# One list-scheduled table for all operations, 64-row projection tiles, Q maxima by a transposing VectorE maximum, and turns by DMA

## The chip, the cores and the metric

The kernel runs on one core of one Trainium2 chip. A core has a matrix engine (TensorE, PE in the profile, with its weight loads shown apart as PEld), a vector engine (VectorE, DVE), a scalar engine (ScalarE, ACT), a general engine (GpSimd, POOL) and a queue engine (SyncE, SP). Each runs its own instructions in order and waits for the others through semaphores. SP and POOL also issue the DMA transfers here; POOL's can change the type on the way, and are used for loads that turn float32 into bf16. Matmul results go to PSUM, eight banks of 128 partitions by 512 float32; everything else lives in SBUF.

The metric is device time in microseconds (us), the median of the runs. Three runs of the kernel before gave 429.13, 429.68 and 428.81.

## The reference

```python
def _attn_ref(q, k, v, w_phi):            # q, k, v: (8 batches, 8 heads, 576 rows, 64)
    def phi(x):                            # w_phi: (64, 128)
        proj = np.einsum('bhsd,df->bhsf', x, w_phi)
        proj = proj - np.max(np.abs(proj), axis=-1, keepdims=True)
        return np.concatenate([np.exp(proj), np.exp(-proj)], axis=-1)
    q_p, k_p = (phi(q), phi(k))
    kv = np.einsum('bhsf,bhsd->bhfd', k_p, v)
    z = np.sum(k_p, axis=2)
    num = np.einsum('bhsf,bhfd->bhsd', q_p, kv)
    den = np.einsum('bhsf,bhf->bhs', q_p, z)[..., None] + 1e-06
    return num / den

def _moe_ref(x, w_gate, w_val, w_out):     # x: (4608, 512), widths 1536
    gate = np.maximum(x @ w_gate, 0.0)
    val = x @ w_val
    return gate * val @ w_out
```

The attention's output, heads side by side, is the input x of the second part (called FFN below). All arrays are float32 in DRAM; the kernel multiplies in bf16.

## The kernel before, in words

**Tiles.** Of the 576 rows of a head, 512 form four chunks of 128 (row p*4+c is partition p of chunk c). The last 64 rows of two neighbouring batches are stacked into one "mixed" tile of 128 partitions. So there are 8 batches of 4 chunks and 4 mixed tiles, 36 x tiles of 128 rows in all, which the FFN takes in 9 groups of 512 rows: one for each batch, and a ninth, `xT_mix`, of the mixed rows.

**Keys.** `k_item` handles one pair of heads. Four 128x128 blocks of k (two chunks of 64 columns side by side) are transposed on PE against `ident` (line 131) and copied out of PSUM by DVE (135). `project_rows` (142) multiplies each transposed block by the 128x256 matrix `w2`, which holds w_phi twice on its diagonal, so that one matmul of 256 columns projects two chunks; half of the products are with zeros. DVE takes the largest absolute value of each row (147, one instruction for 512 columns), ACT makes exp(+proj) and exp(-proj) (177, 512 columns each) and exp of the maxima (184). The maximum isn't subtracted; it scales v instead (`scale_v`, 159 and 165, on POOL). `k_kv` (218) sums k_p^T times [v, 1] over the four chunks and the mixed tile: 20 matmuls of 65 columns for each pair of heads. The mixed tile's foreign half is cut off by `half` (194).

**Queries.** `q_item_chunks` handles two chunks of all heads, `q_item_mixed` a mixed tile. The transposed q (131) is projected twice: by rows through `project_rows`, for nothing but the maxima (142, 147), and by columns in `q_cols` (241), 512 columns to a matmul, for the values that ACT exponentiates into `qp` (247). `q_num` (263) multiplies these by kv in three groups of 3, 3 and 2 heads, 65 columns to a matmul; t = second half times exp(2 max) (279 on DVE, 275 on ACT for two chunks of batch 0), u = first half + t (287), a reciprocal (290), and POOL's product `xu` (292). `q_finish` transposes `xu` on PE (299) and DVE copies it to `xT` (305).

**FFN.** `ffn_slices` yields, for each of 12 blocks of 128 hidden columns, a "val" and a "gate" step of four 512-column matmuls each (320), then 12 "out" steps of four (342). ACT copies val out (329), DVE makes relu(gate) times val (331), ACT copies the output (352) and SP stores it (355; 359 for the mixed group). Group 0 does its first six blocks in halves of 256 columns. One such step of four 512-column matmuls is called a quad below.

**Order.** Every function is entered in a list with a tick, by hand-written formulas, and the list is sorted; an engine does its instructions in that order. Attention of a batch runs about one batch ahead of the FFN, so the last two groups (batch 7 and the mixed one) run with no attention beside them. PSUM is split: five banks for attention (`pa`), three for the FFN (`pf`). POOL issues the loads of k, q and the weights, SP those of v from batch 2 on, and the stores.

```python
        for i in range(2):
            nc.tensor.matmul(
                pp[:, 2 * F * i : 2 * F * (i + 1)],
                lhsT=T2[:, i, :],
                rhs=w2.rearrange("p a f -> p (a f)"),
            )
```

Of the kernel before, what the change touches and what calls it, by code (L numbers as in the profile page):

```python
# [8 lines left out]
FP32 = mybir.dt.float32  # L9
# [3 lines left out]
AX = mybir.AxisListType  # L13


@with_exitstack
def kernel(
# [11 lines left out]

    nc = tc.nc
    B, H, S, D = q.shape
    F = w_phi.shape[1]
    NTOK, DM = out.shape  # L40
    DFF = moe_w_gate.shape[1]
    P = 128
    C = 4
    SF = C * P
    SM = S - SF
    NU = H // 2
    NFC = DFF // P
    NDC = DM // P
    E = D + 1

    ctx.enter_context(nc.allow_low_precision("bf16 matmuls"))
    ctx.enter_context(nc.allow_non_contiguous_dma("strided loads"))

    singles = ctx.enter_context(tc.tile_pool(name="singles", bufs=1))
    sb_in = ctx.enter_context(tc.tile_pool(name="sb_in", bufs=1))
    sb_mix = ctx.enter_context(tc.tile_pool(name="sb_mix", bufs=1))
    sb_T = ctx.enter_context(tc.tile_pool(name="sb_T", bufs=3))
    sb_f = ctx.enter_context(tc.tile_pool(name="sb_f", bufs=3))
    sb_k = ctx.enter_context(tc.tile_pool(name="sb_k", bufs=5))
    sb_kv = ctx.enter_context(tc.tile_pool(name="sb_kv", bufs=14))  # L60
    sb_s = ctx.enter_context(tc.tile_pool(name="sb_s", bufs=6))
    sb_x = ctx.enter_context(tc.tile_pool(name="sb_x", bufs=2))
    sb_h = ctx.enter_context(tc.tile_pool(name="sb_h", bufs=2))
    sb_g = ctx.enter_context(tc.tile_pool(name="sb_g", bufs=4))
    ps_a = ctx.enter_context(tc.tile_pool(name="ps_a", bufs=5, space=bass.MemoryType.PSUM))
    ps_f = ctx.enter_context(tc.tile_pool(name="ps_f", bufs=3, space=bass.MemoryType.PSUM))

    ctx.enter_context(tc.manual_schedule())

    def psum_a(dtype=FP32):  # L70
        n = 512 if dtype == FP32 else 1024
        return ps_a.tile([P, n], dtype, name="pa", tag="pa")

    def psum_f():
        return ps_f.tile([P, 512], FP32, name="pf", tag="pf")

    def load_kqv(b, name, src, eng, dtype, heads):

        t = inputs.get((name, b))
        if t is None:
            t = inputs[name, b] = sb_in.tile([P, H, C, D], dtype, name=f"{name}{b % 2}")
        eng.dma_start(
            out=t[:, heads],
            in_=src[b, heads, 0:SF, :].rearrange("h (p c) d -> p h c d", c=C),
        )

    def load_mixed(i, name, src, eng, dtype):
        t = inputs[name, i] = sb_mix.tile([P, H, D], dtype, name=name)  # L90
        for bb in range(2):
            eng.dma_start(
                out=t[SM * bb : SM * (bb + 1)],
                in_=src[2 * i + bb, :, SF:S, :].rearrange("h p d -> p h d"),
            )

    def load_k(b, lo=0, hi=H):
        load_kqv(b, "kn", k, nc.gpsimd, BF16, slice(lo, hi))

    def load_q(b, lo=0, hi=H):  # L100
        load_kqv(b, "qn", q, nc.gpsimd, BF16, slice(lo, hi))

    def load_v(b, lo=0, hi=H, eng=nc.sync):
        load_kqv(b, "vn", v, eng, FP32, slice(lo, hi))

    inputs = {}
    wg_sb = singles.tile([P, NDC, DFF], BF16)
    wv_sb = singles.tile([P, NDC, DFF], BF16)
    wo_sb = singles.tile([P, NFC, DM], BF16)
    xT_mix = singles.tile([P, NDC, SF], BF16)  # L110
    NS = 3
    SPLIT = NFC // 2

    def load_val_gate(t, w, i):
        n = DFF // NS
        nc.gpsimd.dma_start(
            out=t[:, :, n * i : n * (i + 1)],
            in_=w.rearrange("(c p) n -> p c n", p=P)[:, :, n * i : n * (i + 1)],
        )

    def load_out():
        nc.gpsimd.dma_start(out=wo_sb, in_=moe_w_out.rearrange("(c p) n -> p c n", p=P))

    def transposed(blocks):

        n = len(blocks)
        pt = psum_a(BF16)
        for i, blk in enumerate(blocks):  # L130
            nc.tensor.matmul(  # L131
                pt[:, P * i : P * i + P], lhsT=blk, rhs=ident, is_transpose=True
            )
        t = sb_T.tile([P, n, P], BF16, name=f"tT{n}")
        nc.vector.tensor_copy(t.rearrange("p a b -> p (a b)"), pt[:, 0 : n * P])
        return t

    def project_rows(T2, m):

        pp = psum_a()  # L140
        for i in range(2):
            nc.tensor.matmul(  # L142
                pp[:, 2 * F * i : 2 * F * (i + 1)],
                lhsT=T2[:, i, :],
                rhs=w2.rearrange("p a f -> p (a f)"),
            )
        nc.vector.tensor_reduce(  # L147
            m,
            pp.rearrange("p (c f) -> p c f", f=F),
            axis=AX.X,  # L150
            op=ALU.max,
            apply_absolute_value=True,
        )
        return pp

    def scale_v(engs, dst, src, ek):

        for s, eng in enumerate(engs):
            eng.tensor_tensor(
                dst[:, :, s, 0:D],  # L160
                src,
                ek[:, :, s : s + 1].to_broadcast([P, 8, D]),
                op=ALU.mult,
            )
        engs[0].tensor_copy(dst[:, :, :, D], ek)

    def k_start(st, blocks, pool):
        st["T"] = transposed(blocks)
        st["pool"] = pool
        st["kp"] = []  # L170
        st["m"] = sb_s.tile([P, 8], FP32, name="mk")

    def k_rows(st, i):
        pp = project_rows(st["T"][:, 2 * i : 2 * i + 2], st["m"][:, 4 * i : 4 * i + 4])
        kp = st["pool"].tile([P, 2, 4, F], BF16, name=f"kp{i}")
        for s, sign in ((0, 1.0), (1, -1.0)):
            nc.scalar.activation(
                kp[:, s].rearrange("p c f -> p (c f)"), pp, AF.Exp, scale=sign
            )
        st["kp"].append(kp)  # L180
        if i == 1:
            ek = st["ek"] = sb_s.tile([P, 8, 2], FP32, name="ek")
            for s, sign in ((0, -1.0), (1, 1.0)):
                nc.scalar.activation(ek[:, :, s], st["m"], AF.Exp, scale=sign)

    def k_values(st, b, u, engs):
        vs = st["vs"] = sb_k.tile([P, 8, 2, E], BF16, name="vs")
        vn = inputs["vn", b][:, 2 * u : 2 * u + 2].rearrange("p h c d -> p (h c) d")
        scale_v(engs, vs, vn, st["ek"])

    def k_values_mixed(st, i, bb, engs):

        ekm = sb_s.tile([P, 8, 2], FP32, name="ekm")
        nc.vector.tensor_scalar(
            ekm.rearrange("p a b -> p (a b)"),
            st["ek"].rearrange("p a b -> p (a b)"),
            half[:, bb : bb + 1],
            None,
            op0=ALU.mult,
        )  # L200
        vs = st["vs", bb] = sb_mix.tile([P, 8, 2, E], BF16, name=f"vsm{bb}")
        scale_v(engs, vs, inputs["vm", i], ekm)

    def k_kv(st, b, u, copy):
        mixed = km_state[b // 2]
        pk = psum_a()
        kv_ps = pk[:, 0 : 4 * E].rearrange("p (h s e) -> p h s e", h=2, s=2)
        n = 0
        for hh in range(2):
            h = 2 * u + hh  # L210
            for s in range(2):
                for c in range(C + 1):
                    if c < C:
                        lhsT, rhs = st["kp"][hh][:, s, c, :], st["vs"][:, 4 * hh + c, s, :]
                    else:
                        lhsT = mixed["kp"][h // 4][:, s, h % 4, :]
                        rhs = mixed["vs", b % 2][:, h, s, :]
                    nc.tensor.matmul(  # L218
                        kv_ps[:, hh, s, :], lhsT=lhsT, rhs=rhs, start=(n == 0), stop=(n == 19)
                    )  # L220
                    n += 1
        kv = kvs[b, u] = sb_kv.tile([P, 2, 2, E], BF16, name="kv")
        copy(kv.rearrange("p h s e -> p (h s e)"), pk[:, 0 : 4 * E])  # L223

    def q_start(st, blocks):
        st["T"] = transposed(blocks)
        st["m"] = sb_s.tile([P, 2 * len(blocks)], FP32, name=f"mq{len(blocks)}")

    def q_rows(st, i):
        project_rows(st["T"][:, 2 * i : 2 * i + 2], st["m"][:, 4 * i : 4 * i + 4])  # L230
        if 4 * i + 4 == st["m"].shape[1]:
            st["c"] = sb_s.tile(st["m"].shape, FP32, name="cq")
            nc.scalar.activation(st["c"], st["m"], AF.Exp, scale=2.0)
# [374 lines left out]
```

## Time and profile before

| what | value |
|---|---|
| median of three runs | 429.13 us |
| the profiled execution's span, first to last instruction | 426.3 us |
| PE busy (matmuls with their pipeline time) | 398.7 us, 3357 matmuls |
| DVE busy | 284.1 us, 641 instructions |
| ACT busy | 250.9 us, 575 instructions |
| POOL busy | 159.6 us, 204 instructions |
| first matmul; first FFN matmul; end of the last matmul | 4.46; 31.52; 421.73 us |
| granted TensorE clock, mean | 0.998 |

A matmul's recorded time includes its way through the array, so the recorded times of neighbours overlap. What a matmul costs PE in a row of them is read from the starts in the timeline instead. Where a table of the profile says "idle before", it is the time that the engine stood still just ahead of those instructions, and behind the arrow is what ended the wait.

### The profile page before, as it was taken

The numbers are of one execution on the slowest core, as the hardware profiler recorded it, in microseconds if no ns is written. First come the engines' busy times: TensorE is split into PE (matmuls) and PEld (weight loads), VectorE is DVE, ScalarE is ACT, GpSimd is POOL, SyncE is SP. The second block draws the span as 40 slices with busy tenths as digits, with TensorE's granted clock in tenths as the row PEclk, the third lists the DMA queues.
The fourth block names the chain that finished last, engine by engine and source line by source line (L and its number), as shares of the span: only waits on it lengthen the run. The fifth ranks groups of instructions, "written<-read, shape, count | busy, mean of one in ns | idle before, by whom it ended". The sixth has DMA issues, their size and how long they took to land.

```text
span 426.3 us, 8695 instructions
## 1 busy us (share of the span) xinstructions
PE 398.7 (94%) x3357; PEld 232.9 (55%) x3416; DVE 284.1 (67%) x641; ACT 250.9 (59%) x575; POOL 159.6 (37%) x204
## 2 busy tenths in 40 slices
PE   3777899989999999999999999999999999999995
PEld 1556665645556556555566556555565554444442
DVE  4888569867687679866876699676856795330420
ACT  3984776566667755687567665766667552322321
POOL 8953861176217501574155211870362021000000
PEclk9999999999999999999999999999999999999999
DMA  8997795245413750167015901374020002002004
GB/s 157 199 265 164 108 181 61 75 122 59 56 51 98 128 61 2 61 156 94 2 59 160 116 3 52 71 139 51 26 76 2 1 14 86 2 0 100 0 2 98
DMA packets 45337, 33.66 MB, mean 79 GB/s; under 512 B 12848, under 2 KB 40112, under 8 KB 45296
## 3 DMA queue, kind: packets, MB, share of 16 engines
q0 software_dynamic: 30480, 16.52, 28.1%
q1 hardware_dynamic: 14816, 16.58, 12.4%
q8 instruction: 27, 0.44, 0.4%
q14 instruction: 14, 0.11, 0.1%
HBM read 37.81 MB, written 9.44 MB: 111 GB/s over the span
## 4 chain that ended last, share of the span: by engine, by line
PE 78%; DVE 10%; ACT 4%; POOL 2%; issue 2%; DMA 2%; POOLq 0%; DVEq 0%; ACTq 0%
PE pf L320 40%; PE pf L342 17%; PE pa L142 6%; PE pa L218 5%; PE pa L263 4%; PE pa L241 3%; PE pa L131 3%; DVE u L287 2%; DVE mk L147 2%; DMA qn_117<-in_q_dram 2%; DVE t L279 2%; PE pa L299 1%; POOL xu L292 1%; ACT qp L247 1%; ACT t L275 1%
## 5 line engine op out<-in xcount | busy, mean ns | idle before, releaser
L320 PE MATMUL pf<-xT,wv_sb 128*128 128x512 bf16 (+1 forms) x386 | 96.9, 366 | 3.8 <-DVE xT L305 2.6
L320 PE MATMUL pf<-xT,wg_sb 128*128 128x512 bf16 (+1 forms) x394 | 97.7, 366 | 2.0 <-ACT val_sb L329 1.4
L292 POOL TENSOR_TENSOR xu<-u,r 128x512 bf16<-128x512 f32 x36 | 37.5, 1042 | 164.1 <-DVE r L290 128.9
L329 ACT CAST val_sb<-pf 128x512 bf16<-128x512 f32 (+1 forms) x114 | 65.3, 573 | 52.7 <-PE pf L320 52.3
L247 ACT ACTIVATE qp<-pa 128x512 bf16<-128x512 f32 x128 | 69.5, 604 | 11.9 <-PE pa L241 11.9
L320 PEld LDWEIGHTS <-wg_sb 128*128 128x128 bf16 x456 | 44.4, 98 | 41.6 <-issue 2.1
L320 PEld LDWEIGHTS <-wv_sb 128*128 128x128 bf16 x456 | 43.3, 98 | 36.5 <-issue 3.9
L147 DVE TENSOR_REDUCE mk<-pa 128x4 f32<-128x512 f32 x72 | 48.4, 682 | 11.3 <-PE pa L142 11.1
L263 PEld LDWEIGHTS <-qp 128*128 128x128 bf16 x640 | 33.9, 98 | 21.5 <-issue 0.9
L287 DVE TENSOR_TENSOR u<-pa,t 128x195 f32<-128x195 f32 (+3 forms) x120 | 40.5, 338 | 6.8 <-ACT t L275 0.5
L279 DVE TENSOR_TENSOR t<-pa,cq 128x195 f32<-128x195 f32 (+3 forms) x114 | 37.6, 330 | 4.6 <-PE pa L263 3.8
L352 ACT COPY out_sb<-pf 128x512 f32<-128x512 f32 x36 | 21.3, 592 | 32.4 <-PE pf L342 29.5
L263 PE MATMUL pa<-kv,qp 128*128 128x65 bf16 x640 | 37.9, 193 | 0.9 <-DVE u L287 0.5
L331 DVE SCALAR_TENSOR_TENSOR h_6277<-pf,val_sb 128x512 bf16<-128x512 f32 x12 | 8.3, 692 | 22.8 <-PE pf L320 22.8
L331 DVE SCALAR_TENSOR_TENSOR h_6056<-pf,val_sb 128x512 bf16<-128x512 f32 x12 | 8.3, 692 | 14.5 <-PE pf L320 14.5
L299 PEld LDWEIGHTS <-xu 128*128 128x128 bf16 x144 | 10.7, 98 | 11.7 <-POOL xu L292 3.8
L223 ACT CAST kv<-pa 128x260 bf16<-128x260 f32 x28 | 10.7, 380 | 10.0 <-PE pa L218 9.9
L299 PE MATMUL pa<-ident,xu 128*128 128x128 bf16 x144 | 14.0, 219 | 2.1 <-POOL xu L292 1.6
L331 DVE SCALAR_TENSOR_TENSOR h_566<-pf,val_sb 128x256 bf16<-128x256 f32 (+1 forms) x18 | 9.1, 506 | 8.8 <-ACT val_sb L329 4.1
L331 DVE SCALAR_TENSOR_TENSOR h_1578<-pf,val_sb 128x512 bf16<-128x512 f32 x12 | 8.3, 691 | 9.6 <-ACT val_sb L329 5.7
L305 DVE COPY xT<-pa 128x512 bf16<-128x512 bf16 x32 | 13.3, 417 | 1.9 <-PE pa L299 1.7
L331 DVE SCALAR_TENSOR_TENSOR h_3132<-pf,val_sb 128x512 bf16<-128x512 f32 x12 | 8.2, 686 | 7.3 <-PE pf L320 3.8
(580 smaller groups left out, 776.1 us busy)
## 6 DMA issues: line engine op xcount, KB each, us to landing
out_dram<-out_sb SPq DMA_DIRECT2D x32, 256.0 KB, 2.3
wv_sb<-in_moe_w_val_dram POOLq DMA_DIRECT2D x3, 512.0 KB, 8.2
wg_sb<-in_moe_w_gate_dram POOLq DMA_DIRECT2D x3, 512.0 KB, 9.7
wo_sb<-in_moe_w_out_dram POOLq DMA_DIRECT2D x1, 1536.0 KB, 13.3
vn_1018<-in_v_dram SPq DMA_DIRECT2D x1, 1024.0 KB, 8.9
vn_335<-in_v_dram POOLq DMA_DIRECT2D x1, 1024.0 KB, 13.5
vn_1793<-in_v_dram SPq DMA_DIRECT2D x1, 1024.0 KB, 7.1
vn_2508<-in_v_dram SPq DMA_DIRECT2D x1, 1024.0 KB, 7.2
```

What stands on the lines that cost most here:

```text
L142: nc.tensor.matmul(pp[:, 2 * F * i : 2 * F * (i + 1)], lhsT=T2[:, i, :], rhs=w2.rearrange("p a f -> p (a f)"),)
L147: nc.vector.tensor_reduce(m, pp.rearrange("p (c f) -> p c f", f=F), axis=AX.X, op=ALU.max, apply_absolute_value=True,)
L247: nc.scalar.activation(x["qp"][:, s, slot].rearrange("p a b -> p (a b)"), pf, AF.Exp, scale=sign)
L263: nc.tensor.matmul(pn[:, E * (2 * i + s) : E * (2 * i + s + 1)], lhsT=x["qp"][:, s, slot, blk, :], rhs=kvs[b, h // 2][:, h % 2, s, :],)
L279: nc.vector.tensor_tensor(t, ab[:, :, 1], st["c"][rows, col(lo) : col(lo + n - 1) + 1 : col(1) - col(0)][:, :, None].to_broadcast([np_, n, ...
L287: nc.vector.tensor_tensor(x["u"][rows, lo : lo + n], ab[:, :, 0], t, op=ALU.add)
L292: nc.gpsimd.tensor_tensor(x["xu"], x["u"][:, :, 0:D], r.to_broadcast([P, 8, D]), op=ALU.mult)
L299: nc.tensor.matmul(pt[:, P * i : P * i + P], lhsT=x["xu"][:, 2 * i : 2 * i + 2].rearrange("p a d -> p (a d)"), rhs=ident, is_transpose=True,)
L320: nc.tensor.matmul(ps, lhsT=w[:, dc, P * fi : P * fi + P], rhs=xT[:, dc, lo:hi], start=(dc == 0), stop=(dc == NDC - 1),)
L329: nc.scalar.copy(st["val"], ps)
L331: nc.vector.scalar_tensor_tensor(st["h2"][:, fi, lo:hi], ps, 0.0, st["val"], op0=ALU.max, op1=ALU.mult)
L342: nc.tensor.matmul(st["po"], lhsT=st["h2"][:, fi, P * t : P * t + P], rhs=wo_sb[:, fi, :], start=(fi == 0), stop=(fi == NFC - 1),)
```

## The change

The schedule by ticks is gone. A class `Plan` lists all 1774 operations with a number each; a table `ORDER` gives the order in which they are emitted, and `BANKS` the PSUM bank of each. PSUM is no longer split: four tiles of two neighbouring banks each, given out bank by bank or as a pair. What is computed is the same. The parts:

- **Projections in 64-row tiles.** `wd` holds w_phi once in partitions 0 to 63 and once more in 64 to 127. A projection multiplies only the 64 partitions of one chunk, so the two chunks of a block become two matmuls on separate halves of the rows of the array, which write to the two banks of a pair. They are emitted in turns (first half, second half). For k these are 8 matmuls of 128 columns for each of 36 items, in place of 4 of 256. For q they are 2 of 512 columns for each of 32 visits, in place of 4 of 512 for two visits' worth; batch 0 keeps the full-height `w2` (8 matmuls of 512). Two k items, two q visits, or one of each are done in one go: there are 37 such goes (`tile_visit`).
- **Wider evacuation.** Exponentials and maxima now read both banks of a pair in one instruction: 144 exponentials of 1024 columns (before: 288 of 512) and 36 k maxima of 1024 (before: 72 of 512).
- **Q maxima.** The projection of q by rows (144 matmuls of 256 columns, 72 maxima of 512) is gone. In its place DVE takes the column projection itself: 36 `tensor_reduce` instructions over 1024 columns with `apply_transpose`, which turn each 32x32 square and reduce over 32 features. Behind it a float32 transpose of 128x128 on PE (`CT`, 22), a small DVE maximum over the four parts (`CM`), a DVE transpose (`CX`), and ACT's exp (`CE`).
- **Turns by DMA.** From batch 2 on, k and q of a batch (512 KB of bf16 each) are transposed by one SP DMA each, SBUF to SBUF (12), and so are the x tiles of batches 2 to 7 and three mixed ones (27 of 128 KB). PE keeps 112 bf16 transposes, and batch 0's k comes in as float32 and is transposed as such (20 with the mixed tile). In the table 13 to 21 FFN quads lie between a k turn and its first use, 20 to 34 for q, and 5 to 10 between the last x turn of a batch and the first FFN matmul that reads it.
- **The start.** Batch 0's k and v come on SP's queue as float32, in six pieces, with the mixed k and v among them; POOL's loads wait until the third k piece has landed. Batch 0's q comes in two halves. Group 0 of the FFN works on single chunks of 128 and on 256 columns.
- **Smaller things.** `scale_v` does both signs in one instruction; the mixed tile's v is scaled into rows that were zeroed once, so `half` and line 194 go. The t of line 275 moves from ACT to DVE (`NUM_T`), batch 0's `xu` to DVE. `osb` has 2 buffers (before: 3), xT 3 (2). A v load on SP is let go by a one-element POOL memset into its buffer (`go`).
- **Order.** FFN group b and the attention of batch b+1 are interleaved; behind the last attention matmul the table has the last 11 out quads of group 6, then all of group 7 and of the mixed group.

```diff
+TURNED = (0, 1)
...
+FIRST_SP = (
+    ("kf", 0), ("phi",), ("kf", 1), ("kf", 2), ("kf", 3), ("vf", 0), ("kmf", 0), ("vf", 1), ("vm", 0),
+)
+FIRST_POOL = (
+    ("qn", 0, 0), ("wv", 0), ("wg", 0), ("qn", 0, 1), ("wv", 1), ("wg", 1), ("kn", 1), ("wv", 2), ("wg", 2),
+    ("vn", 1), ("q", 1), ("wo", 0), ("wo", 1), ("wo", 2), ("qm", 0),
+)
+GATE = 2
...
+X_BY_DMA = [(b, c) for b in range(2, B) for c in range(C)] + [("m", i) for i in range(1, B // 2)]
...
+def FFN_PARTS(g, fi):
+    if g == 0:
+        return ((0, 1), (1, 2), (2, 4)) if fi < 6 else ((0, 2), (2, 4))
+    return ((0, 4),)
...
+    def turn(self, tag, src, b):
+        t = self.take(tag, (tag, b), [P, 2 * H, P], BF16)
+        self.nc.sync.dma_start_transpose(out=t, in_=self.has[src, b].rearrange("p h c d -> p (h c d)"))
...
+    def k_rows(self, key):
...
+        w = self.pair((key, "p"))
...
+        for i in range(4):
+            for par in range(2):
+                rows = slice(D * par, D * (par + 1))
+                lo = 512 * par + F * i
+                self.nc.tensor.matmul(w[:, lo : lo + F], lhsT=T[rows, i, :], rhs=self.wd[rows, :])
...
+    def q_cols(self, key, v):
...
+        for par in range(2):
+            rows = slice(D * par, D * (par + 1))
...
+            self.nc.tensor.matmul(
+                w[:, 512 * par : 512 * par + 512].rearrange("p (a b) -> p a b", b=P),
+                lhsT=self.wd[rows, :],
+                rhs=rhs,
+            )
...
+        self.nc.vector.tensor_reduce(
+            dst, src, axis=AX.X, op=ALU.max, apply_absolute_value=True, apply_transpose=True
+        )
...
+    def c_turn(self, key):
+        self.nc.tensor.matmul(
+            self.bank((key, "pc"))[:, 0:P], lhsT=self.has[key, "R"], rhs=self.ident_f, is_transpose=True
+        )
...
+    def c_max(self, key):
+        M = self.take("M", (key, "M"), [P, 32], FP32)
+        self.nc.vector.tensor_reduce(
+            M, self.bank((key, "pc"))[:, 0:P].rearrange("p (f t) -> p t f", f=4), axis=AX.X, op=ALU.max
+        )
...
+    def c_back(self, key):
+        MT = self.take("MT", (key, "MT"), [P, 32], FP32)
+        self.nc.vector.transpose(MT, self.has[key, "M"])
...
+    def x_by_dma(self, xk):
+        self.nc.sync.dma_start_transpose(
+            out=self.x_place(xk), in_=self.has[xk, "xu"].rearrange("p h d -> p (h d)")
+        )
...
+    ops = Plan().ops
+    banks = iter(BANKS)
+    for i in ORDER.split():
+        o = ops[int(i)]
+        for _, key in o.psum:
+            emit.bank_of[key] = int(next(banks))
+        getattr(emit, o.call[0])(*o.call[1:])
```

## The prediction

> **What bounds the kernel.** First the engines' busy time and the chain of work that ended last:
>
> ```profile
> PE 398.7 (94%) x3357; PEld 232.9 (55%) x3416; DVE 284.1 (67%) x641; ACT 250.9 (59%) x575; POOL 159.6 (37%) x204
> ...
> PE 78%; DVE 10%; ACT 4%; POOL 2%; issue 2%; DMA 2%; POOLq 0%; DVEq 0%; ACTq 0%
> ```
>
> PE is busy nearly always and carries the chain. Then the stretches before the first FFN matmul, up to 60 us, up to the end of attention, and the rest (length, then busy time by engine):
>
> ```profile
> 0.00:31.50 31.50, 18.48 (x198) 12.66 (x201) 21.58 (x49) 22.70 (x63) 24.40 (x37) 1.00 1.13 204
> 31.50:60.00 28.50, 24.26 (x282) 18.71 (x284) 19.96 (x48) 19.29 (x53) 19.54 (x26) 1.00 0.89 152
> 60.00:355.00 295.00, 289.52 (x2575) 171.44 (x2623) 224.07 (x516) 189.03 (x428) 114.60 (x142) 1.00 0.35 68
> 355.00:427.00 72.00, 66.41 (x306) 30.05 (x310) 18.53 (x30) 19.92 (x34) 1.04 (x1) 0.98 0.14 41
> ```
>
> Between 60 and 355 us PE is idle 5.5 us of 295, so there a matmul less is its time less; DVE has 76%. In the first 31.5 us PE waits for loads and short chains. Now the price of each matmul, from the timeline of PE (start, length, line): starts, not lengths, count.
>
> ```profile
> 136.88 0.29 PE L218 MATMUL pa<-vs,kp_2254 128*128 128x65 bf16 x4
> ...
> 137.48 0.38 PE L142 MATMUL pa<-w_119,tT_2359 128*128 128x256 bf16 x2
> 137.70 1.03 PE L320 MATMUL pf<-xT,wv_sb 128*128 128x512 bf16 x4
> 138.57 0.38 PE L142 MATMUL pa<-w_119,tT_2359 128*128 128x256 bf16 x2
> ...
> 139.65 0.61 PE L131 MATMUL pa<-ident,qn_1874 128*128 128x128 bf16 x8
> 140.10 0.81 PE L320 MATMUL pf<-xT,wv_sb 128*128 128x512 bf16 x3
> ```
>
> Twenty 65-column matmuls of kv took 0.60 us (0.030 each; those of `q_num`, six in 0.19, 0.032), two of 256 columns 0.22 (0.109), four of 512 0.864 (0.216, mean of such rows), eight transposes 0.45 (0.056). PE's demand before: FFN 1296 x 0.216 = 279.9; transposes 432 x 0.056 = 24.2; row projections 288 x 0.109 = 31.4; column projections 72 x 0.216 = 15.6; kv 640 x 0.030 = 19.2; num 640 x 0.032 = 20.5. Sum 390.8. The span of 426.3 has 35.5 more: by 31.5 us some 11.4 of work are done (36 transposes, 36 row and 7 column projections, 80 kv, 32 num, 8 x transposes), so 20.1 are lost at the start; 4.6 pass after the last matmul; 10.8 lie between.
>
> **PE's new demand.** Row projections of q (144 x 0.109) vanish. FFN, kv and num stay: 319.6. Bf16 transposes: 112 x 0.056 = 6.3. The 42 float32 ones aren't in the trace: below, 0.056 as for bf16 of the same shape; above, 0.216, the longest row; I take twice 0.056, being nearest to the same shape with twice the bytes: 4.7 (2.4 to 9.1). Projections in half-height tiles aren't there either: if the halves run side by side, k costs 36 x 4 x 0.056 = 8.1 and q 32 x 0.216 = 6.9; if one after the other, 16.1 and 13.8. I take side by side, since they use different rows and different banks. Batch 0's 8 full ones: 1.7. Sum 347.3, so 43.5 less than before (bounds 345 to 367).
>
> A second price is the change of tiling, 37 goes, in and out: 74 times. Below: nothing. Above: the array runs empty, 379 ns (a 512-column matmul alone) less 216 (in a row) = 163 ns, 12.1 us. I take half, 6.0, having no row nearer to either end. The Trainium skill speaks against this change here: "TensorEngine Tiling (Array Packing)", Key Properties, says that changing the tiling mode drains the engine. No run here shows it; by that rule the forecast would be 6 us later, without it 6 earlier.
>
> **DVE and ACT.** The groups by shape:
>
> ```profile
> L147 DVE TENSOR_REDUCE mk<-pa 128x4 f32<-128x512 f32 x72 | 48.4, 682 | 11.3 <-PE pa L142 11.1
> L247 ACT ACTIVATE qp<-pa 128x512 bf16<-128x512 f32 x128 | 69.5, 604 | 11.9 <-PE pa L241 11.9
> L287 DVE TENSOR_TENSOR u<-pa,t 128x195 f32<-128x195 f32 x64 | 23.0, 361 | 4.6 <-ACT t L275 0.5
> L331 DVE SCALAR_TENSOR_TENSOR h_566<-pf,val_sb 128x256 bf16<-128x256 f32 x12 | 5.0, 419 | 5.6 <-ACT val_sb L329 4.1 <-PE pa L299 0.8 <-PE pa L142 0.7
> L331 DVE SCALAR_TENSOR_TENSOR h_3878<-pf,val_sb 128x512 bf16<-128x512 f32 x12 | 8.2, 685 | 6.5 <-PE pf L320 4.3 <-ACT val_sb L329 1.6 <-PE pa L131 0.6
> ```
>
> DVE takes 266 ns for 256 more columns, 1.04 ns each, so a maximum of 1024 costs 682 + 512 x 1.04 = 1214 ns, against two of 682. The turning one isn't in the trace: below, 1214; above, twice that, if each square is passed twice. I take 1214, the row of the same operation on the same operand. DVE after: maxima 72 x 1.214 = 87.4; gates 96 x 0.685 + 18 x 0.419 + 12 x 0.29 (by the slope) = 76.8; t and u 80 x 0.713 + 40 x 0.575 = 80.0; copies of transposed blocks 28 x 0.417 + 4 x 0.69 = 14.4; reciprocals 7.3; `CM` and `CX` 22 x 0.5 (estimate: 128 and 32 columns on the same slope) = 11; kv copies, batch 0's xu and v 8.5. Sum 285: unchanged, since what the copies save goes into t, xu and the small steps. ACT: an exponential of 512 costs 69.5/128 = 543 ns in a row, one of 1024 543 + 512 x 0.773 (594 and 396 ns for vals of 512 and 256) = 939, so 144 x 0.939 = 135 against 288 x 0.543 = 156; about 229 in all. POOL's products are as many elements as before; its loads and the memsets leave it far under half.
>
> These hide under PE, but less well. After attention come 83 quads, 71.7 us of PE alone. In the 313 us ahead of them (the forecast's) DVE has 285 less 24 x 0.685 = 269, 86% against 76%.
>
> **The DMA turns** of k, q and x aren't in the trace. Rows of like size:
>
> ```profile
> vn_1793<-in_v_dram SPq DMA_DIRECT2D x1, 1024.0 KB, 7.1
> ...
> out_dram<-out_sb SPq DMA_DIRECT2D x8, 128.0 KB, 2.4
> ...
> vm<-in_v_dram SPq DMA_DIRECT2D x6, 128.0 KB, 6.9
> ...
> qn_1099<-in_q_dram POOLq DMA_DIRECT2D x1, 512.0 KB, 10.0
> ```
>
> (KB, then us from issue to landing.) A 512 KB turn: 3.6 (half of 7.1) to 10.0 us, I take 7; 13 quads ahead of the first use are 11.2 us, so nothing waits. A 128 KB x turn: 2.4 to 6.9, against 5 to 10 quads, 4.3 to 8.6 us. At 6.9 groups 2, 3, 6 and 7 start 1.7, 2.6, 0.9 and 1.7 late, 7 us in all; at 2.4 nothing; I take 3.5. On SP's queue a k turn also waits for its load, which is issued 4 to 10 quads (3.5 to 8.6 us) earlier and lands after 6 to 8; behind it stand the q turn and the next x turns and stores, for some 3 us, and an out copy with only two buffers waits for a store. That is hidden while x turns keep their slack; without it the x figures grow by the same 3 us in the groups named.
>
> **The start.** SP brings 2560 KB, at the 204 GB/s of the first window 12.8 us alone; with q's first half and the first weights beside it (another 2560 KB) 25. I take 17 for the last piece, the mixed v. From its product to the first FFN matmul took 9.1 us before (22.4 to 31.5); the new chain has the same steps but the t on ACT, I take 8. First FFN matmul at 25 (21 to 31); PE has done 9.4 by then (20 float32 transposes 2.2, 5 goes 1.1, 16 transposes 0.9, kv 2.4, 6 projections 1.3, num 1.0, the rest 0.5), so 15.6 are lost (11 to 20).
>
> **The sum.** PE 347.3; changes of tiling 6.0; start 15.6; idle between, 10.8 x 86/76 = 12.2 plus 3.5 for late x, 16 (10.8 to 25); after the last matmul 4.6. A span of 389.5. The median before stands 2.8 above the profiled span (429.13 less 426.3), so **392**. All low ends: 345 + 0 + 11 + 10.8 + 4.6 + 2.8 = 374. All high ends, with the halves side by side: 352 + 12 + 20 + 25 + 4.6 + 2.8 = 416.
>
> **Rivals.**
> *Halves one after the other* (PE serialises tiles): + 8.0 + 6.9, 407. For it: nothing in the trace runs two matmuls at once. Against: different rows, different banks.
> *DVE becomes the bound* (the turning maximum takes twice): 36 x 1.214 = 43.7 more, 313 of DVE in attention's 313. DVE stood idle 9.9 us of the first 31.5 and 8.5 up to 60, so that phase takes some 331, and the whole 331 + 71.7 + 4.6 + 2.8 = 410. For it: its chains already ended PE's waits (u, t, mk in the chain). Against: half the price is taken by no other reduce here.
> *The turns bind, slower than before.* SP's turns run one behind the other, three 512 KB for each of batches 2 to 7 (k, q, four x). Attention's phase may last until 429.1 - 2.8 - 4.6 - 71.7 = 350 before the gain is gone; (350 - 60) / 6 = 48 us to a batch, so from 16 us a turn (32 GB/s) the kernel is slower; at 21 us it is 60 + 6 x 63 + 79 = 517. For it: a new kind of transfer, and DMA is busy only in bursts now. Against: the slowest 512 KB row is 10.0. The Trainium skill bears on this: "VectorE: DVE Perf Modes", The three transpose paths, gives 1309 ns for a 128x128 bf16 block by DMA. An estimate by it, 16 blocks in sequence, is 21 us, which would make it slower; no run here shows it, and the sum goes by the rows.
> *The order misses*, engines in order on wrong guesses: idle between doubles to 32, 408.
>
> **How the numbers follow.** Forecast 0.55 (its own range 374 to 402); halves in sequence 0.10; DVE 0.13; order 0.08; turns 0.10 (over 429); a better start and no stalls, under 374, 0.04. The range 374 to 418 leaves out the turns, that last case and a share of DVE's. A difference under 0.2% can't be told from none: faster 0.88, same 0.01, slower 0.11.
>
> **What would show it.** Right: row projections by q gone, starts of paired matmuls a few ns apart, idle PE between 60 us and the end of attention near 4%, DVE near 86% there, first FFN matmul near 25 us, 512 KB turns landing within 10 us. Wrong: PE idle behind DMA turns at each group's first matmul; DVE without gaps; 160 ns holes around each go; a maximum of q over 2 us.

## The result, and the profile after

The changed kernel takes 474.79 us (median; 472.42 to 475.97). The kernel before, run beside it, takes 429.4. The ratio is 1.104, interval 1.0995 to 1.1083: 45 us slower, where 37 faster was forecast.

The profile after: busy time by engine, and the chain of work that ended last.

```profile
PE 388.3 (82%) x3234; PEld 207.3 (44%) x3234; DVE 265.2 (56%) x574; ACT 242.3 (51%) x430; POOL 147.3 (31%) x171
...
PE 41%; DVE 12%; ACT 11%; issue 3%; DVEq 0%; ACTq 0%
```

Every engine has less to do than before (PE 398.7, DVE 284.1, ACT 250.9) and the span is longer: no engine has become the bound. The chain can be followed back only to 154 us here, so its shares add up to 67% of the span; of that part PE has some 60%, DVE 18 and ACT 16 (before: PE 78, DVE 10 and ACT 4 of 98%). The stretches up to 60 us, up to the last attention matmul, and the rest (start and end, length, busy time of PE, PEld, DVE, ACT and POOL, then granted clock, DMA share and GB/s):

```profile
0.00:60.00 60.00, 36.61 (x418) 28.68 (x419) 44.38 (x101) 27.21 (x53) 24.77 (x38) 0.77 0.98 170
60.00:392.00 332.00, 276.69 (x2490) 146.57 (x2488) 202.34 (x442) 193.96 (x342) 120.45 (x131) 1.00 0.51 92
392.00:473.00 81.00, 74.98 (x331) 32.03 (x329) 18.43 (x32) 21.10 (x36) 2.09 (x2) 0.98 0.15 43
```

In the middle stretch, where PE was idle 5.5 us of 295 before, it is now idle 55.3 of 332 (17%; forecast 4%). All other engines have gaps there too: DVE is busy 61% of it, ACT 58%. So no engine is busy throughout, and each waits for others. Which waits? From the list of waits (engine and line <- what ended the wait: us in total, times, longest):

```profile
ACT val L988 <- PE W L976: 77.4, 67, 4.2
...
PEld L976 <- issue: 47.6, 88, 1.8
...
DVE mk L716 <- ACT kp L730: 31.8, 16, 5.0
...
ACT qp L860 <- DVE R L854: 18.9, 16, 5.9
DVE R L854 <- ACT qp L860: 17.3, 17, 3.7
ACT val L988 <- DVE u L932: 13.9, 7, 3.7
ACT kp L730 <- DVE mk L716: 13.4, 12, 1.3
PE W L976 <- DVE h L993: 13.4, 21, 1.1
ACT osb L1015 <- DVE u L932: 11.0, 3, 4.9
```

Two kinds stand out. The maxima (`mk`, `R`) and the exponentials (`kp`, `qp`) wait for each other, in both directions. And ACT's copy `val` of an FFN result, like its copy `osb` of the output, waits for `u`, a DVE sum of the attention. These share no data. One such wait, first on DVE's timeline (start, length), then on ACT's (in brackets the wait ahead of it):

```profile
190.23 0.81 DVE L932 TENSOR_TENSOR u<-W,t 128x195 f32<-128x195 f32 x3
```

```profile
190.96 0.59 ACT L988 CAST val<-W 128x512 bf16<-128x512 f32 x1 [3.65 <-DVE u L932]
```

The copy starts as the third sum ends, having stood 3.65 us. What the two have in common is in the code: `bank()` hands out halves of four two-bank tiles. If dependences between instructions are recorded by PSUM tile, an instruction on one bank waits for earlier ones on its neighbour. The built program has such waits: of the semaphore waits between two of PE, ACT and DVE, 354 are for an instruction that touches only the other bank of the tile and shares no other data (238 of them PE's); in the kernel before, where each buffer is a tile of its own, there are none.

That gives theory 1, false waits between the two banks of a tile. Theory 2: the waits come from the wide readers, which occupy both banks of a pair while exponential, maximum and exponential take turns. Theory 3: the fixed order doesn't fit the durations, whatever the tiles.

### The profile page after: what moved, and what is told of

Its sections match the earlier page's. It is cut to its first block, busy times and chain, and to the rows that moved or that the text cites. A ratio compares the mean times of both kernels' runs of the same rounds, so it can differ in the third digit from the quotient of the medians.

```text
span 472.9 us, 8269 instructions
## 1 busy us (share of the span) xinstructions
PE 388.3 (82%) x3234; PEld 207.3 (44%) x3234; DVE 265.2 (56%) x574; ACT 242.3 (51%) x430; POOL 147.3 (31%) x171
## 4 chain that ended last, share of the span: by engine, by line
PE 41%; DVE 12%; ACT 11%; issue 3%; DVEq 0%; ACTq 0%
PE W L976 24%; PE W L1005 13%; DVE h L993 4%; DVE R L854 3%; ACT kp L730 3%; ACT qp L860 3%; ACT val L988 2%; PE W L904 2%; DVE u L932 2%; DVE mk L716 2%; DVE t L927 1%; ACT osb L1015 1%; PE W L777 1%; PE W L712 0%; ACT ek L727 0%
## 5 line engine op out<-in xcount | busy, mean ns | idle before, releaser
L993 DVE SCALAR_TENSOR_TENSOR h<-W,val 128x512 bf16<-128x512 f32 (+2 forms) x126 | 76.5, 609 | 100.6 <-PE W L976 62.9
L988 ACT CAST val<-W 128x512 bf16<-128x512 f32 (+2 forms) x126 | 66.0, 526 | 108.6 <-PE W L976 77.4
L976 PE MATMUL W<-xT,wv 128*128 128x512 bf16 (+2 forms) x456 | 102.6, 348 | 18.2 <-DVE h L993 8.4
L976 PE MATMUL W<-xT,wg 128*128 128x512 bf16 (+2 forms) x456 | 102.5, 348 | 11.2 <-DVE h L993 5.0
L1005 PE MATMUL W<-wo,h 128*128 128x512 bf16 x432 | 99.8, 379 | 7.6 <-ACT osb L1015 3.7
L860 ACT ACTIVATE qp<-W 128x1024 bf16<-128x1024 f32 x72 | 72.8, 1030 | 27.2 <-DVE R L854 18.9
L740 POOL TENSOR_TENSOR vs<-vn,ek 128x1024 bf16<-128x1024 f32 (+1 forms) x34 | 59.6, 1752 | 68.5 <-ACT ek L727 44.4
L730 ACT ACTIVATE kp<-W 128x1024 bf16<-128x1024 f32 x64 | 64.6, 1025 | 23.0 <-DVE mk L716 13.4
L976 PEld LDWEIGHTS <-wv 128*128 128x128 bf16 x504 | 47.3, 99 | 61.4 <-issue 25.2
L976 PEld LDWEIGHTS <-wg 128*128 128x128 bf16 x504 | 47.2, 99 | 59.6 <-issue 22.5
L854 DVE TRANSPOSE_TENSOR_REDUCE R<-W 128x32 f32<-128x1024 f32 x36 | 43.6, 1236 | 17.3 <-ACT qp L860 17.3
```

Of the source, the lines that this page charges most:

```text
L730: self.nc.scalar.activation(self.has[key, "kp"][:, s].rearrange("p c f -> p (c f)"), self.pair((key, "p")), AF.Exp, scale=(1.0, -1.0)[s],)
L740: eng.tensor_tensor(dst[:, :, :, 0:D], src.unsqueeze(1).to_broadcast([n, ns, nh, D]), ek.unsqueeze(3).to_broadcast([n, ns, nh, D]), op=ALU ...
L854: self.nc.vector.tensor_reduce(dst, src, axis=AX.X, op=ALU.max, apply_absolute_value=True, apply_transpose=True)
L860: self.nc.scalar.activation(self.has[vk, "qp"][:, s].rearrange("p a b -> p (a b)"), self.pair((vk, "p")), AF.Exp, scale=(1.0, -1.0)[s],)
L976: self.nc.tensor.matmul(ps, lhsT=w[:, dc, P * fi : P * fi + P], rhs=xT[:, dc, P * lo : P * hi], start=(dc == 0), stop=(dc == NDC - 1),)
L988: self.nc.scalar.copy(t[:, 0:n], self.bank((k, "v", "p"))[:, 0:n])
```

## The experiments

| run | median us | ratio to before, interval |
|---|---|---|
| `e1_bank` dependences by bank | 422.19 | 0.9823 (0.9798 to 0.9849) |
| `b_pair` kernel before, two buffers to a tile | 691.77 | 1.6107 (1.6077 to 1.6138) |
| `b_fixed` kernel before, fixed buffers, a tile each | 432.08 | 1.0059 (1.0041 to 1.0077) |
| `e_split` one-bank tiles, readers of 512 columns | 405.07 | 0.9443 (0.9387 to 0.9499) |
| `e_split2` the same again | 407.81 | 0.9461 (0.943 to 0.9492) |
| `e_norow` no 64-row tiles | 410.87 | 0.9547 (0.9517 to 0.9576) |
| `e_dve` POOL silent for DVE's first scalings | 420.53 | 0.9794 (0.9777 to 0.981) |
| `e_pool` all scalings on POOL | 420.13 | 0.9785 (0.9771 to 0.98) |
| `e_warm` 56 extra matmuls, placed too late | 423.89 | 0.9866 (0.9847 to 0.9884) |
| `e_warm2` the same, placed as meant | 423.98 | 0.9846 (0.9813 to 0.988) |
| `e_best` `e_split` with scalings on POOL | 406.88 | 0.9445 (0.9418 to 0.9473) |
| `e_late_w` `e_best` with later weights | 408.15 | 0.9504 (0.9486 to 0.9521) |

**Dependences by bank.** Instructions, order, tiles and banks stay as in the changed kernel; each PSUM access only declares that it doesn't depend on accesses to the other bank.

```diff
+    def log(self, r, aps, kw):        # for every instruction that touches a tile W
...
+            for other, ob, orest in old[-120:]:
+                if other.engine == me.engine:
+                    continue
+                if not (ob & banks) and not (orest & rest):
+                    self.tc.declare_no_dep(me, other, reason="other bank")
```

> The changed kernel with one thing taken out: the dependence between accesses to the two different banks of one two-bank PSUM tile (instructions, their order, tiles and bank numbers stay). Theory 1 (the two-bank tiles make every access to a bank wait for the accesses to its neighbour, so that eight banks act as four): the lost time falls by most of what the forecast missed; 395 to 425 us, faster than before, idle of TensorE between 80 and 400 us from some 50 down to 20 us or less. Theory 2 (the three 1024-column readers of a pair take turns, as two engines may not read one bank at once): these waits stay, so 450 us or more, with the waits of max on exp and exp on max as large as now. Theory 3 (the fixed order itself does not fit the durations): 455 us or more.

422.19 us: 52.6 less than the changed kernel, and now faster than before. None of the 354 waits is left in its program. The three stretches:

```profile
0.00:60.00 60.00, 39.72 (x440) 31.41 (x441) 47.16 (x106) 29.73 (x61) 26.28 (x39) 1.00 0.97 170
60.00:345.00 285.00, 266.18 (x2467) 142.40 (x2466) 195.08 (x433) 189.83 (x334) 118.95 (x131) 1.00 0.59 107
345.00:421.00 76.00, 71.37 (x331) 32.19 (x329) 19.30 (x36) 21.12 (x36) 2.09 (x2) 1.00 0.16 46
```

The same attention work now ends at 345 instead of 392; PE's idle time in it fell from 55.3 to 18.8 us. No copy waits for a `u` any more, and PE's waits are short (list of waits):

```profile
DVE mk L774 <- ACT kp L788: 27.4, 16, 4.0
...
ACT qp L918 <- DVE R L912: 22.8, 21, 6.1
...
DVE R L912 <- ACT qp L918: 19.6, 20, 3.3
...
ACT kp L788 <- DVE mk L774: 14.4, 12, 1.5
...
PE W L1034 <- DVE h L1051: 3.9, 8, 0.7
PE W L1034 <- ACT val L1046: 3.7, 5, 1.5
```

Theory 3 is out as the main cause: the order is unchanged. The waits between readers are as large as ever; theory 2 foresaw that, but not the time.

**The suspected cost put into the other kernel.** The kernel before has none of the change's parts. Its eight buffers were laid out two to a tile; a control has the same fixed buffers as eight tiles.

```diff
+    W = [ps.tile([P, 1024], FP32, name=f"W{i}") for i in range(4)]
+    banks = [W[i // 2][:, 512 * (i % 2) : 512 * (i % 2) + 512] for i in range(8)]
```

> The kernel before with its eight one-bank PSUM buffers laid two to a tile (five buffers of the attention and three of the FFN as before, same order and instructions). Theory 1: the false waits alone slow it by 5% or more, 450 us or more. Theories 2 and 3: it has none of the wide readers and keeps its own order, so it stays within 2%, under 438 us.

> Control for the run with paired buffers: the kernel before with the same eight fixed buffers, each a tile of its own. Every theory: within 1% of before, 425 to 434 us; were it slower, the fixed rotation and not the pairing would be what the paired run shows.

Control 432.08; paired 691.77, 60% more, with the same instructions in the same order. Paired, its waits read (PE stands 222 us of 690):

```profile
DVE h L336 <- PE W L325: 153.6, 91, 13.1
ACT val_sb L334 <- PE W L325: 127.0, 80, 5.9
ACT kp L182 <- DVE mk L152: 104.4, 65, 6.6
```

In the control the same three are 66.4, 54.7 and 48.3 us. The false waits cost far more here than in the changed kernel; why the two differ so much is open. Theory 1 is shown from both sides.

**Readers of one bank.** Eight one-bank tiles need no declaration, but no instruction can then span two banks. Each wide exponential and maximum is cut in two; the paired matmuls and the order stay.

```diff
+        self.W = [ps.tile([P, 512], FP32, name=f"W{i}") for i in range(8)]
...
+        for a, w in enumerate(self.pair((key, "p"))):
+            self.nc.scalar.activation(
+                self.has[key, "kp"][:, s].rearrange("p c f -> p (c f)")[:, 512 * a : 512 * a + 512],
+                w, AF.Exp, scale=(1.0, -1.0)[s])
```

> The changed kernel with eight one-bank PSUM tiles, each 1024-column exp and maximum of a pair cut into two of 512 columns (order, banks and the paired 64-row matmuls stay). Theory 1: no false waits are left, so it comes near the run with dependences by bank (422 us): 415 to 435 us, the doubled count of readers costing ACT some 20 us and DVE some 10 us of busy time that TensorE mostly covers. Rival (the wide readers themselves are worth the time, or their number and not the tiles makes the waits): 450 us or more. If the turns of ACT and DVE on one bank were a large part of what is left over the forecast, it would come out below 415.

405.07 us, and 407.81 when run again. Theory 1 gave 415 to 435; below 415 was to mean that the turns of ACT and DVE on one bank are a large part of what is left. It is 14 to 17 less than with wide readers and the same freedom between banks. The groups by line, ACT then DVE, show what it paid:

```profile
L866 ACT ACTIVATE qp<-W 128x512 bf16<-128x512 f32 x144 | 78.6, 607 | 14.8 <-PE W L836 8.5 <-DVE R L854 5.5 <-DVE t L933 0.5
```

```profile
L854 DVE TRANSPOSE_TENSOR_REDUCE R<-W 128x16 f32<-128x512 f32 x72 | 46.0, 690 | 10.1 <-ACT qp L866 10.0
```

Against the changed kernel's `qp` (72 of 1030 ns, 72.8 us) and `R` (36 of 1236, 43.6), both are busy longer, but they wait less for each other, since each holds one bank and leaves the other free:

```profile
DVE mk L717 <- ACT kp L732: 21.1, 15, 3.9
...
DVE R L854 <- ACT qp L866: 10.0, 14, 2.5
```

`R` waits 10.0 us for exponentials instead of 19.6, `qp` for `R` 5.5 instead of 22.8. So theory 2 holds for a second, smaller part; false waits can't be that part, as `e1_bank` has none left. The Trainium skill has the rule behind it ("PSUM — Partial Sum Buffer", PSUM bank collisions raise a hardware error): no two engines may touch the same bank and partitions at once, reads against reads included, while different banks are free. Both kernels order such readers, so no run here shows it; by that rule the wait within one bank can't be left out. The stretches now:

```profile
0.00:60.00 60.00, 41.73 (x487) 32.87 (x488) 47.83 (x123) 35.50 (x93) 28.02 (x42) 0.80 0.96 171
60.00:328.50 268.50, 260.80 (x2419) 139.55 (x2419) 196.78 (x490) 195.29 (x447) 116.39 (x127) 1.00 0.63 113
328.50:405.00 76.50, 71.67 (x333) 32.30 (x330) 18.95 (x35) 21.11 (x36) 2.09 (x2) 1.00 0.16 45
```

PE is idle 7.7 of 268.5 us, 3%, while attention runs.

**No 64-row tiles**, on this base: the same number of matmuls over all 128 rows, with the zero-padded weight.

```diff
-  ... lhsT=T[rows, i, :], rhs=self.wd[rows, :])
+  ... lhsT=T[:, i, :], rhs=self.w2[:, par, :])
-                lhsT=self.wd[rows, :],
+                lhsT=self.w2[:, par, :],
```

> The run with one-bank tiles again, beside the runs that are built on it, so that they share a chip. Every theory: 402 to 408 us.

> The run with one-bank tiles, with the 64-row projections made 128-row ones again: the same count of matmuls, each over all 128 rows with the weight padded by zeros for the other half, so that no two run side by side and no tiling changes in batches 1 to 7 (results unchanged). If the pairs run side by side and a change of tiling costs nothing: 288 row matmuls at 55 instead of 36 ns and 64 column matmuls at 207 instead of 140 ns, TensorE +5.5 and +4.3, so about 10 us slower than its base. If the 74 changes of tiling cost the forecast's 6.0 us: about 4 us slower. If the halves run one after the other (the first rival of the prediction): the same or faster.

410.87 against 407.81; by the ratios 3.7 us slower (1 to 6). One go on PE's timeline, in `e_split2` and then in `e_norow`:

```profile
163.19 2.75 PE L1011 MATMUL W<-wo,h 128*128 128x512 bf16 x12
165.88 0.62 PE L712 MATMUL W<-wd,kT 64*128 64x128 bf16 x16
```

```profile
301.88 1.06 PE L712 MATMUL W<-w,kT 128*128 128x128 bf16 x16
302.77 0.28 PE L874 MATMUL W<-ident_f,R 128*128 128x128 f32 x1
```

Twelve matmuls at 216 ns are 2.59 us, but the go starts 2.69 after them: the change of tiling costs 0.10 us. Over 25 goes that follow matmuls of 512 columns the median is 96 ns; in `e_norow` there is no such gap. In `e_split2` a go of 16 row matmuls lasts 0.55 us and one of 8 lasts 0.32, so a pair takes 57 ns, as long as one matmul of full height (0.89 us for sixteen in `e_norow`), and the change back takes the other 0.09. Four column matmuls take 0.54 and two 0.32: 0.22 a pair. So the pairs do run side by side, which saves about 15 us (144 x 57 and 32 x 215 ns), and 74 changes at 0.1 us take about 7 of them back. Of the 8 that are left 3.7 (1 to 6) reach the time; where the rest goes is open.

**The start.** With the waits gone, the first FFN matmul still comes at 39.4 us in `e1_bank` and 35.8 in `e_split`; 25 was forecast. Four edits, each of one suspect. First DVE's scaling of v beside POOL (`SCALE_V` alone differs):

> The run with dependences by bank, with the two scalings of the first v pieces (third unit and second mixed half) that POOL did beside DVE moved to DVE, so that POOL computes nothing from 19 to 27 us. Theory 5a (DVE's scaling takes 3.8 us for 64x1024 and 2.3 us for 128x512 because POOL works beside it; the same form took 0.68 us with POOL idle): these fall to about 1.4 and 0.7 us, the first FFN matmul comes 2 to 4 us earlier, 416 to 421 us. Theory 5b (the size of these operations is their own): DVE gets 3 to 6 us more in the chain, 423 to 430 us.

> The run with dependences by bank, with the three scalings at the start that DVE did moved to POOL. Theory 5a and 5b: DVE is free some 6 us earlier for the query maxima, while POOL's own chain grows by about 4.5 us; 418 to 424 us. If the first FFN matmul still comes at 39 us, the start is set by the chain of k and q visits and not by DVE's scaling.

DVE's timeline, first with dependences by bank, then with POOL silent:

```profile
19.31 3.78 DVE L798 TENSOR_TENSOR vsm<-vm,ek 64x1024 bf16<-64x1024 f32 x1
...
23.75 2.26 DVE L798 TENSOR_TENSOR vs<-vn,ek 128x512 bf16<-128x512 f32 x1
...
28.09 0.68 DVE L798 TENSOR_TENSOR vs<-vn,ek 128x512 bf16<-128x512 f32 x1
```

```profile
19.27 1.22 DVE L798 TENSOR_TENSOR vsm<-vm,ek 64x1024 bf16<-64x1024 f32 x1
...
21.16 0.68 DVE L798 TENSOR_TENSOR vs<-vn,ek 128x512 bf16<-128x512 f32 x1
```

The operation is three times as slow with POOL at work beside it. The first FFN matmul comes 2.2 us earlier, the time is 1.7 us less; with POOL doing it all, 2.1 (the intervals of all three overlap, and the two executions of one kernel, `e_split` and `e_split2`, have that matmul 2.0 us apart, at 35.8 and 37.8). Next, TensorE's speed: until 42 us its matmuls of 128 columns start 107 ns apart, later 55. Extra matmuls were to keep it awake (`lhsT=rhs=ident`, 56 of them, overwritten later).

> The run with dependences by bank, with 56 more 128-column bf16 matmuls ahead of the first key-value products, into the bank that these overwrite, so that TensorE is busy without a break from about 16 to 22 us, where it waits for ACT and DVE otherwise. Theory 4a (TensorE at half speed until 42 us is what delays the first FFN matmul): full speed from about 20 us, as in the kernel before; matmuls of 128 columns at 55 ns instead of 107 from there; 2 to 8 us less, 414 to 420 us. Theory 4b (the start is set by ACT and DVE taking turns, with DVE's scaling in the middle): TensorE is faster but waits longer, 421 to 424 us.

> The run with dependences by bank and the 56 extra matmuls, now ahead of the first key-value products that the order has, where TensorE waits from 16.3 to 23.3 us (in the run before they stood at 25.5 us, in the way of other work). Theory 4a (half speed of TensorE delays the start): full speed from about 20 us, 2 to 6 us less, 416 to 420 us. Theory 4b (ACT and DVE set the start): within 1.5 us of 422.

In the first try the extra matmuls ran at 25.5 us, in the way. In the second they filled 20.0 to 25.8, and PE's timeline shows full speed behind them, and half speed again later:

```profile
25.84 0.29 PE L840 MATMUL W<-vs,kp 128*128 128x65 bf16 x4
25.97 0.19 PE L840 MATMUL W<-vsm,kpm 128*128 128x65 bf16 x1
26.00 0.29 PE L840 MATMUL W<-vs,kp 128*128 128x65 bf16 x4
...
40.92 0.63 PE L1039 MATMUL W<-xT,wg 128*128 128x128 bf16 x4
41.35 0.63 PE L1039 MATMUL W<-xT,wv 128*128 128x128 bf16 x4
```

Five matmuls of 65 columns in 0.16 us, then four of 128 in 0.43. The first FFN matmul came at 40.5, the time was 423.98: no gain (a little outside 4b's 1.5 us, but its interval overlaps that of `e1_bank`). As the speed fell again by 33.5 us, the run doesn't show what full speed up to the first FFN matmul would bring. Last, the two gains together, and the transfers:

> One-bank tiles together with all scalings of the start on POOL: the two gains found, 17 and 2 us against the run with dependences by bank, add up: 401 to 405 us, first FFN matmul 1 to 3 us before the 35.8 us of its base. If the split has already taken the waits that the scaling made: the same as its base within 1 us.

> The run with one-bank tiles and all scalings of the start on POOL (406.9 us, first FFN matmul at 36.4), with the first three weight transfers of the FFN (512 KB each) issued by POOL after its fourth scaling, at about 16 us, instead of from 7.5 us on. Theory 6a (the start is set by the transfers: the 128 KB of mixed v take 10.5 us to 17.4 us because the queues move 200 GB/s without a break): the mixed v is there by 14 us, the mixed scaling starts 3 us earlier, the first FFN matmul 2 to 4 us earlier, 402 to 405 us. Theory 6b (weights are needed early, or the chain of visits sets the start): the first FFN matmul at 36 us or later, 406 us or more.

The scalings on POOL add nothing that can be told to `e_split` (406.88 against 407.81, intervals overlap). Later weights bring none either: 408.15, first FFN matmul at 36.5, because POOL issues them ahead of the mixed scaling, which then starts at 18.5 instead of 17.9. No single one of these suspects holds the start. The chain of `e_best` (start, length) shows where it is longer than forecast:

```profile
6.95 10.47 DMA vm<-in_v_dram
...
17.91 1.35 POOL vsm L742
...
36.44 2.25 PE W L982 x20
```

The last piece, the mixed v, lands at 17.4 us, as forecast (17). From the start of its product to the first FFN matmul it is 18.5 us, where 8 were given. In this run POOL's scalings and transfer issues fill the first 10.0 of them; with DVE doing some of the scalings it was no shorter (19.4 to 39.65 in the changed kernel). What would shorten it stays open.

## Why the prediction was wrong, point by point

**The step that failed** is "idle between, 10.8 x 86/76 = 12.2 plus 3.5 for late x, 16 (10.8 to 25)". It took the idle time from DVE's load, as if an instruction waited only for its own data. After the change PE stood 55.3 us between 60 us and the last attention matmul alone. The four two-bank tiles and their halves stood in the change, but what a wait is recorded for was not asked. Dependences by bank took away 52.6 us of the 82.8 that the forecast missed. With them PE's idle time in that phase was 18.8, within the range that the step gave; this is in part luck, as DVE, from whose 86% the step was worked out, was busy 68%.

**Second, the wide readers** were priced by their own length, and nearly rightly. Their groups in the changed kernel (busy time, mean ns of one, idle time before and what ended it):

```profile
L860 ACT ACTIVATE qp<-W 128x1024 bf16<-128x1024 f32 x72 | 72.8, 1030 | 27.2 <-DVE R L854 18.9
...
L716 DVE TENSOR_REDUCE mk<-W 128x8 f32<-128x1024 f32 x36 | 42.9, 1220 | 39.7 <-ACT kp L730 31.8
...
L854 DVE TRANSPOSE_TENSOR_REDUCE R<-W 128x32 f32<-128x1024 f32 x36 | 43.6, 1236 | 17.3 <-ACT qp L860 17.3
```

A maximum was forecast at 1214 ns, turning or not, an exponential at 939. What was left out is the last column: they hold both banks while the other engine waits: another 14 to 17 us. Cut in two they cost more busy time and less time.

**Third, the start.** "First FFN matmul at 25 (21 to 31)": 39.65 after the change, 35.8 to 37.8 with one-bank tiles. The term that was mis-sized is "the new chain has the same steps but the t on ACT, I take 8": 18.5 in `e_best`, 20.3 in the changed kernel. With one-bank tiles the first FFN matmul is 11 to 13 us late, about as much as is left between 405 to 408 and the forecast's 392 (13 to 16); that it passes into the time in full is not shown. The scaling beside POOL explains some 2 of them.

**What held.** PE's demand: the row projections of q are gone, and a pair of halves takes as long as one matmul, 57 and about 215 ns, as was assumed. PE's idle share was 7% without the false waits and 3% with the readers cut as well (forecast near 4%). The changes of tiling take about 7 us, where 6.0 was put down as half of an upper bound; that it came so near is luck. No PE wait on a turn by DMA appears in the list of waits. The turns themselves:

```profile
xT<-xu SPq DMA_TRANSPOSE x24, 2.5
...
kT<-kn SPq DMA_TRANSPOSE x6, 11.6
qT<-qn SPq DMA_TRANSPOSE x6, 4.9
```

(Count, then median us from issue to landing.) A k turn takes longer than the 10.0 given, at the edge of the 11.2 of its cover; q and x are within. The prediction's estimate from the Trainium skill's "VectorE: DVE Perf Modes", The three transpose paths, 21 us for a turn, was far too long. DVE was busy 61% of the attention's phase and 73% with one-bank tiles, not 86; it had 265 us to do, where 285 was forecast.

**The rivals.** None was it. DVE was not the bound, the turns didn't bind, the halves ran side by side. "The order misses" is nearest in its sign, since idle time grew, but the order was kept in the runs that took it away. The case that came, slower by a wait between things that share no data, had no place among them.

## What to carry to other kernels

When buffers are merged into a larger tile, ask what the waits are recorded for: if by tile, each use of one part waits for the other, and eight buffers act as four. In a list of waits the sign is an engine waiting for an instruction that shares no data with it. An instruction that reads two banks saves a fixed cost and holds both; where two engines take turns on them, the shorter one can be the faster one: one-bank tiles with twice the readers gave the best time here, 405 to 408 us, against 429 before.

## What the runs showed of the hardware

- DVE's product of two SBUF operands took 3.78 us beside POOL's and 1.22 without (64x1024), 2.26 and 0.68 (128x512). The Trainium skill's "SBUF — State Buffer", SBUF: two separate sides, tells of one port pair that these two engines lock for a whole instruction; the trace agrees: DVE's cast of 64x16 behind the first product took 0.21 us in `e1_bank`, 1.21 in `e_split` and 2.64 in `e_split2`, the long ones beside POOL's products.
- From about 15 us on TensorE ran at half speed (107 ns between matmuls of 128 columns, 55 later) until 44 us in the changed kernel, but for a microsecond at 29, and until 42 in `e1_bank`, though the latter's row of granted clock shows full speed throughout. In `e_warm2` it sped up under 6 us of unbroken matmuls (20.0 to 25.8) and was slow again by 33.5, within 8 us of sparse ones.
- A change between 64-row and 128-row tiles cost about 0.1 us each way on PE (`e_split2`), and two 64-row matmuls on separate halves took as long as one of 128 rows.
- Turns of equal size differ: 11.6 us for k, 4.9 for q, on the same queue.
